# Attention feeding a mixture of experts: expert stages issued in a staggered order, and a normalization moved from VectorE to ScalarE

## The chip, the cores and the metric

The kernel runs on one core of a Trainium2 chip. A core has TensorE (PE in the profile; its weight loads are the row PEld), VectorE (DVE), ScalarE (ACT), GpSimd (POOL), SyncE (SP, which here only issues transfers) and 16 DMA engines. Engines run in parallel; each takes its own instructions strictly in order, and waits on semaphores for what it needs. The metric is the device time of one execution in microseconds (us), lower is better. One execution is profiled; the others are only timed.

## The reference, cut to what matters

First an attention with 8 batches, 8 heads, 576 positions and 64 channels: a coarse attention on positions averaged in groups of four, repeated four times, plus a local one in a band of |i-j| < 4. Then each of the 4608 tokens (512 channels) goes through the two matrices of its own expert, one of 8.

```python
out_d = sm_attn(q_d, k_d, v_d)                # means over 4 positions
out_up = np.repeat(out_d, factor, axis=2)
...
return (out_up + out_local).astype(np.float32)

def _moe_ref(x, domain_id, w1, w2):           # N, D, E, F = (4608, 512, 8, 1024)
    for e in range(E):
        mask = domain_id == e
        h = np.maximum(x[mask] @ w1[e], 0.0)
        out[mask] = h @ w2[e]
```

## The kernel before

**Routing** (lines 81 to 126, then 148 to 154). Every token gets a position in a list with 768 places per expert. Thirty-six indirect transfers on POOL's queue write the list to DRAM (`hx_idx`). Places that stay empty point at a row of zeros.

**Attention** (`_attn_head_pair`, 32 calls: 8 batches by 4 pairs of heads). POOL's queue loads q, k and v and casts them to fp16 on the way; SP's queue loads v in fp32 as well. PE transposes q and k (lines 260, 261) and forms the sums over four positions (lines 272, 274); copies marked `nc.any` (lines 262 to 277) go to ACT or DVE as the build decides. PE multiplies q by k, ACT takes the exponentials (lines 325 to 330), DVE applies the band mask (line 346), and PE multiplies by v, with a column of ones that yields the denominators. In lines 351 to 359 DVE takes the reciprocal of the coarse denominators (`odr`) and multiplies the coarse result `od_ps` by it, giving `odnp`: four multiplications a pair of heads, two of 128x64 and two of 16x64. ACT's queue stores `odnp` to DRAM (lines 368, 369). DVE does the same for the local part (lines 373 to 386), and SP's queue stores it to the bridge tensor `hx_bridge`. After each second batch `_od_add_pass` loads both parts, adds them on DVE and stores the sum; its transfers are on ACT's queue. In PSUM the tags `tr`, `ds` and `sx` have two buffers each. `ds` is shared in turn by the position sums (`pdt_ps`, `pdtl_ps`), the coarse scores (`pd_ps`) and the coarse results (`od_ps`), so an `od_ps` must be read before the next pair's position sums can be written.

**Experts** (lines 163 to 175). For expert e, `_moe_gather` issues on POOL's queue the loads of both weight matrices (1 MB each in fp16, read as 2 MB in fp32) and six indirect gathers of 128 tokens from `hx_bridge` into `xg`; the index tile `idxt` comes over SP's queue. `_moe_compute` has three parts: 24 PE transposes into `xt_ps` and four ACT copies into `xt` (call it T); 64 matmuls in eight groups, each group ended by an ACT Relu into `ht` (H); and six output groups of eight matmuls, each followed by an ACT copy into `o_sb` and an indirect scatter of 128 rows to the output on POOL's queue (O for the matmuls, S for the scatters; S.0 to S.5). The loop gathers for e+1, then computes e.

What is held how often: `idxt`, `xg`, `xt`, `ht` and `o_sb` have three buffers, the weights two, `h_ps` two, `xt_ps` and `o_ps` one. So gather e+3 needs the `idxt` of expert e back, which the last scatter of e still reads; the copy into `o_sb` number four waits for the first of its three buffers. All 48 scatters write the one tensor `out`, so each waits for the one before to have landed.

The order in each engine's queue is fixed when the program is built: among instructions that the builder takes to be ready, the one that comes first in the source is issued first, and others fill the gaps. So an engine's order is not simply the source order: in the profile the transposes of the next expert already lie between output groups of the current one.

Of the kernel before, what the change touches and what calls it, by code (L numbers as in the profile page):

```python
# [11 lines left out]
FP16 = mybir.dt.float16  # L12
I32 = mybir.dt.int32
AF = mybir.ActivationFunctionType
P = 128
CAPJ = 6
# [12 lines left out]
def kernel(  # L29
# [10 lines left out]
    nc = tc.nc  # L40

    B, H, S, D = q.shape
    NTOK = B * S
    DM = H * D
    E, _, F = moe_w1.shape
# [15 lines left out]
        name="h_ltri",  # L61
# [18 lines left out]
    with tc.tile_pool(name="prep_ps", bufs=2, space=bass.MemoryType.PSUM) as pps:  # L80
# [47 lines left out]
    with (  # L128
        tc.tile_pool(name="acon", bufs=1) as acon,
        tc.tile_pool(name="asb", bufs=5) as asb,  # L130
        tc.tile_pool(name="aps", bufs=1, space=bass.MemoryType.PSUM) as aps,
    ):
        id16a = acon.tile([P, P], FP16, name="id16a")
        nc.sync.dma_start(id16a[:], identh_c[:])
        mask5_s = acon.tile([P, 5, P], FP16, name="mask5_s")
        nc.sync.dma_start(mask5_s[:], mask5_c[:])

        for b in range(B):
            for hj in range(H // 2):
                _attn_head_pair(  # L140
                    nc, q, k, v, xdr, odb, b, 2 * hj,
                    asb, aps, id16a, mask5_s,
                    scale_local, scale_ds, S, D, SD, NSPAN, DM,
                )
            if b % 2 == 1:
                _od_add_pass(nc, xdr, odb, b - 1, S, SD, DM, asb)

    for t in range(NT):
        nc.gpsimd.indirect_dma_start(  # L149
            out=idxd[:],  # L150
            out_offset=bass.IndirectOffsetOnAxis(ap=pos_s[:, t : t + 1], axis=0),
            in_=tok_s[:, t : t + 1],
# [3 lines left out]
    with (  # L156
        tc.tile_pool(name="mcon", bufs=1) as mcon,
        tc.tile_pool(name="mw", bufs=2) as mw,
        tc.tile_pool(name="msb", bufs=3) as msb,
        tc.tile_pool(name="mhp", bufs=1, space=bass.MemoryType.PSUM) as mhp,  # L160
        tc.tile_pool(name="mop", bufs=1, space=bass.MemoryType.PSUM) as mop,
    ):
        id16 = mcon.tile([P, P], FP16, name="id16")
        nc.sync.dma_start(id16[:], identh_c[:])
        pre = [None] * E
        pre[0] = _moe_gather(nc, 0, moe_w1, moe_w2, xdr, idxd, mw, msb, DM, F)
        for e in range(E):
            if e + 1 < E:
                pre[e + 1] = _moe_gather(
                    nc, e + 1, moe_w1, moe_w2, xdr, idxd, mw, msb, DM, F  # L170
                )
            _moe_compute(
                nc, e, out, mhp, mop, msb, id16, DM, F, NTOK, *pre[e]
            )
            pre[e] = None


def _od_add_pass(nc, xdr, odb, b0, S, SD, DM, pool):
# [35 lines left out]
def _attn_head_pair(  # L214
# [66 lines left out]
    with nc.allow_low_precision(reason="sums of 4 fp16 pooled values"):  # L281
        nc.vector.tensor_reduce(
            out=vd65[:, :, 0:D],
            in_=vq[:].rearrange("p r hh d -> p hh d r"),
# [3 lines left out]
            out=vdl65[:, :, 0:D],  # L288
            in_=vql[:].rearrange("p r hh d -> p hh d r"),
# [33 lines left out]
    for hh in range(2):  # L323
        ed[hh] = asb.tile([P, 2, SD], FP16, name=f"ed{hh}", tag=f"ed{hh}")
        nc.scalar.activation(out=ed[hh][:, 0, :], in_=pd_ps[hh][:, 0, :],
                             func=AF.Exp, scale=scale_ds)
        nc.scalar.activation(out=ed[hh][0:16, 1, :], in_=pd_ps[hh][0:16, 1, :],
                             func=AF.Exp, scale=scale_ds)
        el[hh] = asb.tile([P, NSPAN, P], FP16, name=f"el{hh}", tag=f"el{hh}")
        nc.scalar.activation(out=el[hh][:], in_=sc_ps[hh][:], func=AF.Exp,  # L330
                             scale=scale_local)

    od_ps = [None, None]
# [15 lines left out]
    odnp = asb.tile([P, 2, 2, D], FP16, name="odnp")  # L349
    for hh in range(2):  # L350
        odr = asb.tile([P, 2, 1], FP32, name=f"odr{hh}", tag=f"odr{hh}")
        nc.vector.reciprocal(odr[:, 0, :], od_ps[hh][:, 0, D : D + 1])
        nc.vector.reciprocal(odr[0:16, 1, :], od_ps[hh][0:16, 1, D : D + 1])
        nc.vector.tensor_scalar_mul(
            odnp[:, 0, hh, :], od_ps[hh][:, 0, 0:D], odr[:, 0, :]
        )
        nc.vector.tensor_scalar_mul(
            odnp[0:16, 1, hh, :], od_ps[hh][0:16, 1, 0:D], odr[0:16, 1, :]
        )
        xl_ps[hh] = aps.tile([P, NSPAN, D + 1], FP32, name=f"xl_ps{hh}",  # L360
                             tag="sx", bufs=2)
        for t in range(NSPAN):
            nc.tensor.matmul(
                xl_ps[hh][:, t, :], pl[hh][:, t, :], vh[:, t, hh, :],
                start=True, stop=True,
            )
# [4 lines left out]
    for hh in range(2):  # L371
# [4 lines left out]
            out=xw[:, 0:4, hh, :],  # L376
# [5 lines left out]
            out=xw[0:96, 4, hh, :],  # L382
# [19 lines left out]
def _moe_gather(nc, e, moe_w1, moe_w2, xdr, idxd, mw, msb, DM, F):  # L402
    NDC = DM // P
    NFC = F // P
    w1e = mw.tile([P, NDC, F], FP16, name="w1e")
    nc.gpsimd.dma_start(w1e[:], moe_w1[e].rearrange("(dc p) f -> p dc f", p=P))  # L406
    w2e = mw.tile([P, NFC, DM], FP16, name="w2e")
    nc.gpsimd.dma_start(w2e[:], moe_w2[e].rearrange("(fc p) d -> p fc d", p=P))
    base = e * CAPJ * P
    idxt = msb.tile([P, CAPJ], I32, name="idxt")  # L410
    nc.sync.dma_start(
        idxt[:], idxd[base : base + CAPJ * P, 0].rearrange("(j p) -> p j", p=P)
    )
    xg = msb.tile([P, CAPJ, DM], FP16, name="xg")
    for j in range(CAPJ):
        nc.gpsimd.indirect_dma_start(  # L416
            out=xg[:, j, :],
            out_offset=None,
            in_=xdr[:],
            in_offset=bass.IndirectOffsetOnAxis(ap=idxt[:, j : j + 1], axis=0),  # L420
        )
    return (w1e, w2e, idxt, xg)


def _moe_compute(nc, e, out, mhp, mop, msb, id16, DM, F, NTOK, w1e, w2e, idxt, xg):
    NDC = DM // P
    NFC = F // P
    NCOL = CAPJ * P

    xt_ps = mhp.tile([P, NDC, NCOL], FP16, name="xt_ps", tag="xt_ps")  # L430
    for j in range(CAPJ):
        for u in range(NDC):
            nc.tensor.transpose(  # L433
                xt_ps[:, u, bass.ts(j, P)], xg[:, j, bass.ts(u, P)], id16[:]
            )
    xt = msb.tile([P, NDC, NCOL], FP16, name="xt")
    for u in range(NDC):
        nc.scalar.copy(out=xt[:, u, :], in_=xt_ps[:, u, :])  # L438

    ht = msb.tile([P, NFC, NCOL], FP16, name="ht")  # L440
    for fc in range(NFC):
        h_ps = mhp.tile([P, NCOL], FP32, name="h_ps", tag="h_ps", bufs=2)
        for dc in range(NDC):
            lhs = w1e[:, dc, bass.ts(fc, P)]
            nc.tensor.matmul(  # L445
                h_ps[:, 0:512], lhs, xt[:, dc, 0:512],
                start=(dc == 0), stop=(dc == NDC - 1),
            )
            nc.tensor.matmul(  # L449
                h_ps[:, 512:NCOL], lhs, xt[:, dc, 512:NCOL],  # L450
                start=(dc == 0), stop=(dc == NDC - 1),
            )
        nc.scalar.activation(out=ht[:, fc, :], in_=h_ps[:], func=AF.Relu)  # L453

    for j in range(CAPJ):
        o_ps = mop.tile([P, DM], FP32, name="o_ps", tag="o_ps")
        for fc in range(NFC):
            nc.tensor.matmul(  # L458
                o_ps[:], ht[:, fc, bass.ts(j, P)], w2e[:, fc, :],
                start=(fc == 0), stop=(fc == NFC - 1),  # L460
            )
        o_sb = msb.tile([P, DM], FP32, name="o_sb", tag="o_sb")
        nc.scalar.copy(out=o_sb[:], in_=o_ps[:])  # L463
        nc.gpsimd.indirect_dma_start(  # L464
            out=out[:],
            out_offset=bass.IndirectOffsetOnAxis(ap=idxt[:, j : j + 1], axis=0),
            in_=o_sb[:],
            in_offset=None,
            bounds_check=NTOK - 1,
            oob_is_err=False,  # L470
        )
# [30 lines left out]
```

## Time and profile before

| | |
|---|---|
| median of 6 runs | 692.96 us (689.18 to 694.49) |
| the profiled execution | 690.53 us, span 688.8 us |
| PE busy | 494.7 us, 72% |
| POOL busy | 334.7 us, 49% |
| ACT busy | 267.9 us, 39% |
| DVE busy | 237.0 us, 34% |
| mean granted TensorE clock | 0.945 of full |
| routing on PE and DVE, before the first pair of heads | 0 to 69 us |
| attention, 32 pairs of heads | 69 to 378 us |
| last additions to the bridge, first gather | 378 to 407 us |
| experts | 407 to 689 us |

A group's line gives the source line, the engine, the operation, output and input tiles, shapes and count, then busy time and mean duration, and after a second bar the idle time of the engine just ahead of these instructions with what ended it. A timeline's line gives start and duration in us, engine and line, and in brackets the idle time before and its releaser. In a list of waits each line says who waited for whom: the total in us, how many times, and the longest. ACTq and SPq mark instructions that only issue a transfer; they take their place in the engine's order.

### The profile page before, as it was taken

To read this page: it belongs to the slowest core of one execution; us is meant where nothing else is said; L and a number is where in the kernel's file an instruction comes from. 1 tells how busy PE (TensorE), PEld (TensorE's weight loads), DVE (VectorE), ACT (ScalarE), POOL (GpSimd) and SP (SyncE) were. 2 spreads that over 40 slices of the span, in tenths; PEclk is the share of its full clock that TensorE was granted. 3 is DMA by queue.
4 is the path that set the end of the run, shared out by engine and by line. 5 is a ranking of instruction groups with operands and counts; after the bars stand their busy time and mean duration, and the time that the engine had idled before them with its cause. 6 is when DMAs were issued, how large, how long until landed. Compare 5 with 4: busy or idle time off the path is not lost. (4 is left out here: it accounts for less than half of the span.)

```text
span 688.8 us, 10101 instructions
## 1 busy us (share of the span) xinstructions
PE 494.7 (72%) x3352; PEld 300.7 (44%) x3352; DVE 237.0 (34%) x1118; ACT 267.9 (39%) x528; POOL 334.7 (49%) x408
## 2 busy tenths in 40 slices
PE   1888989976997658867997029874939294867993
PEld 1777656543654435534554025441515152433441
DVE  2664455775667736668567100000000000000000
ACT  0100756435763345634664014531514241433541
POOL 9930667675976659955000255234252434343222
PEclk9999999999999999999999999996969788796997
DMA  9990669999999989999214597355565545364411
GB/s 118 180 83 1 52 86 105 149 143 144 100 143 170 152 106 85 131 201 181 34 29 111 147 211 169 99 86 138 90 137 101 122 95 88 111 113 121 92 50 53
DMA packets 226905, 77.93 MB, mean 113 GB/s; under 512 B 196609, under 2 KB 218898, under 8 KB 226836
## 3 DMA queue, kind: packets, MB, share of 16 engines
q0 software_dynamic: 133504, 46.71, 55.1%
q1 hardware_dynamic: 72100, 15.23, 12.9%
q10 hardware_dynamic: 21248, 15.35, 7.9%
q8 instruction: 26, 0.43, 0.3%
q14 instruction: 27, 0.22, 0.1%
HBM read 88.09 MB, written 23.37 MB: 162 GB/s over the span
## 5 line engine op out<-in xcount | busy, mean ns | idle before, releaser
L458 PE MATMUL o_ps<-w2e,ht 128*128 128x512 f16 x384 | 100.8, 410 | 71.1 <-ACT o_sb L463 69.7
L464 POOL DMA_INDIRECT out_dram<-o_sb,idxt x48 | 47.3, 986 | 118.1 <-ACT o_sb L463 45.1
L458 PEld LDWEIGHTS <-ht 128*128 128x128 f16 x384 | 39.7, 103 | 120.8 <-issue 88.9
L445 PE MATMUL h_ps<-xt,w1e 128*128 128x512 f16 x256 | 89.0, 394 | 1.6 <-ACT xt L438 1.0
L463 ACT COPY o_sb<-o_ps 128x512 f32<-128x512 f32 x48 | 28.1, 586 | 138.0 <-DMA out_dram<-o_sb,idxt 70.0
L416 POOL DMA_INDIRECT xg<-hx_bridge,idxt x48 | 46.3, 964 | 63.4 <-DMA idxt<-hx_idx 47.3
L449 PE MATMUL h_ps<-xt,w1e 128*128 128x256 f16 x256 | 72.1, 282 | 0.0
L230 POOL DMA_DIRECT2D vq<-in_v_dram x32 | 58.4, 1836 | 13.9 <-DVE pos_s L125 9.5
L230 POOL DMA_DIRECT2D qn<-in_q_dram x32 | 48.1, 1504 | 33.5 <-PE pdtl_ps L274 22.2
L453 ACT ACTIVATE ht<-h_ps 128x768 f16<-128x768 f32 x64 | 51.8, 811 | 29.4 <-PE h_ps L449 29.2
L149 POOL DMA_INDIRECT hx_idx<-tok_s,pos_s x36 | 37.8, 1049 | 48.9 <-DMA hx_idx<-tok_s,pos_s 44.4
L230 POOL DMA_DIRECT2D kn<-in_k_dram x32 | 50.4, 1575 | 2.3 <-PE pdtl_ps L274 2.3
L234 POOL DMA_DIRECT2D vql<-in_v_dram x32 | 41.5, 1297 | 2.4 <-DVE qt L265 1.6
L262 ACT COPY qt<-tr_ps 128x512 f16<-128x512 f16 x24 | 31.1, 1298 | 28.8 <-PE tr_ps L260 28.8
L234 POOL DMA_DIRECT2D knl<-in_k_dram x32 | 40.9, 1278 | 0.0
L445 PEld LDWEIGHTS <-w1e 128*128 128x128 f16 x256 | 25.9, 101 | 32.8 <-issue 4.7
L249 ACT CAST vh<-vn 128x640 f16<-128x640 f32 x32 | 23.1, 727 | 42.9 <-DVE vn L247 21.5
L433 PE MATMUL xt_ps<-id_6095,xg 128*128 128x128 f16 x192 | 15.7, 230 | 31.0 <-DMA xg<-hx_bridge,idxt 31.0
L438 ACT COPY xt<-xt_ps 128x768 f16<-128x768 f16 x32 | 24.0, 816 | 35.5 <-PE xt_ps L433 35.5
L117 PE MATMUL p_rank<-p_oh,ltri_s 128*128 128x8 f32 x72 | 21.4, 371 | 21.9 <-DVE p_oh L108 21.9
L406 POOL DMA_DIRECT2D w1e<-in_moe_w_dram x8 | 6.7, 844 | 62.0 <-DMA hx_bridge<-oax 62.0
L234 POOL DMA_DIRECT2D qnl<-in_q_dram x32 | 36.5, 1139 | 0.7 <-PE pdtl_ps L274 0.7
(1787 smaller groups left out, 1113.0 us busy)
## 6 DMA issues: line engine op xcount, KB each, us to landing
vn<-in_v_dram SPq DMA_DIRECT2D x64, 128.0 KB
w1e<-in_moe_w_dram POOLq DMA_DIRECT2D x8, 1024.0 KB, 8.5
w2e<-in_moe_w_dram POOLq DMA_DIRECT2D x8, 1024.0 KB, 9.9
oax<-hx_bridge ACTq DMA_DIRECT2D x36, 128.0 KB
hx_bridge<-oax ACTq DMA_DIRECT2D x36, 128.0 KB
qn<-in_q_dram POOLq DMA_DIRECT2D x32, 128.0 KB, 6.5
kn<-in_k_dram POOLq DMA_DIRECT2D x32, 128.0 KB, 6.3
vq<-in_v_dram POOLq DMA_DIRECT2D x32, 128.0 KB, 7.2
```

What stands on the lines that cost most here:

```text
L149: nc.gpsimd.indirect_dma_start(out=idxd[:], out_offset=bass.IndirectOffsetOnAxis(ap=pos_s[:, t : t + 1], axis=0), in_=tok_s[:, t : t + 1], ...
L230: nc.gpsimd.dma_start(dst[:], src[b, hA : hA + 2, 0:512, :].rearrange("h (p r) d -> p r h d", r=4),)
L234: nc.gpsimd.dma_start(dstl[:], src[b, hA : hA + 2, 512:S, :].rearrange("h (p r) d -> p r h d", r=4),)
L262: nc.any.tensor_copy(tt[:, 0:512].rearrange("w (p r) -> w r p", r=4), ps_m[:])
L416: nc.gpsimd.indirect_dma_start(out=xg[:, j, :], out_offset=None, in_=xdr[:], in_offset=bass.IndirectOffsetOnAxis(ap=idxt[:, j : j + 1], ax ...
L438: nc.scalar.copy(out=xt[:, u, :], in_=xt_ps[:, u, :])
L445: nc.tensor.matmul(h_ps[:, 0:512], lhs, xt[:, dc, 0:512], start=(dc == 0), stop=(dc == NDC - 1),)
L449: nc.tensor.matmul(h_ps[:, 512:NCOL], lhs, xt[:, dc, 512:NCOL], start=(dc == 0), stop=(dc == NDC - 1),)
L453: nc.scalar.activation(out=ht[:, fc, :], in_=h_ps[:], func=AF.Relu)
L458: nc.tensor.matmul(o_ps[:], ht[:, fc, bass.ts(j, P)], w2e[:, fc, :], start=(fc == 0), stop=(fc == NFC - 1),)
L463: nc.scalar.copy(out=o_sb[:], in_=o_ps[:])
L464: nc.gpsimd.indirect_dma_start(out=out[:], out_offset=bass.IndirectOffsetOnAxis(ap=idxt[:, j : j + 1], axis=0), in_=o_sb[:], in_offset=Non ...
```

## The change

Two things. First, `_moe_compute` is split into `_moe_phaseA` (T), `_moe_phaseB` (H) and `_moe_phaseC` (O and S), and the loop issues A of expert e, then C of expert e-1, then B of expert e; the last C follows the loop. Tiles, pools, shapes and the number of instructions stay; `ht` is now created at the end of A. Second, the four multiplications a pair that form `odnp` become ACT activations with the function Copy and the reciprocal as a scale per partition.

```diff
+        sA = [None] * E
         pre[0] = _moe_gather(nc, 0, moe_w1, moe_w2, xdr, idxd, mw, msb, DM, F)
         for e in range(E):
             if e + 1 < E:
                 pre[e + 1] = _moe_gather(
                     nc, e + 1, moe_w1, moe_w2, xdr, idxd, mw, msb, DM, F
                 )
-            _moe_compute(
-                nc, e, out, mhp, mop, msb, id16, DM, F, NTOK, *pre[e]
-            )
-            pre[e] = None
+            sA[e] = _moe_phaseA(nc, e, mhp, msb, id16, DM, F, *pre[e])
+            if e >= 1:
+                _moe_phaseC(nc, e - 1, out, mop, msb, DM, F, NTOK, *sA[e - 1])
+                sA[e - 1] = None
+            _moe_phaseB(nc, e, mhp, DM, F, *sA[e])
+        _moe_phaseC(nc, E - 1, out, mop, msb, DM, F, NTOK, *sA[E - 1])
...
-        nc.vector.tensor_scalar_mul(
-            odnp[:, 0, hh, :], od_ps[hh][:, 0, 0:D], odr[:, 0, :]
-        )
-        nc.vector.tensor_scalar_mul(
-            odnp[0:16, 1, hh, :], od_ps[hh][0:16, 1, 0:D], odr[0:16, 1, :]
+        nc.scalar.activation(
+            out=odnp[:, 0, hh, :], in_=od_ps[hh][:, 0, 0:D], func=AF.Copy,
+            scale=odr[:, 0, :],
+        )
+        nc.scalar.activation(
+            out=odnp[0:16, 1, hh, :], in_=od_ps[hh][0:16, 1, 0:D], func=AF.Copy,
+            scale=odr[0:16, 1, :],
         )
...
-def _moe_compute(nc, e, out, mhp, mop, msb, id16, DM, F, NTOK, w1e, w2e, idxt, xg):
+def _moe_phaseA(nc, e, mhp, msb, id16, DM, F, w1e, w2e, idxt, xg):
...
     ht = msb.tile([P, NFC, NCOL], FP16, name="ht")
+    return (w1e, w2e, idxt, xt, ht)
+
+
+def _moe_phaseB(nc, e, mhp, DM, F, w1e, w2e, idxt, xt, ht):
...
+def _moe_phaseC(nc, e, out, mop, msb, DM, F, NTOK, w1e, w2e, idxt, xt, ht):
```

More of the change, by code (lines that the diff above doesn't have):

```diff
@@ L440, in _moe_compute @@
     ht = msb.tile([P, NFC, NCOL], FP16, name="ht")
+    return (w1e, w2e, idxt, xt, ht)
+def _moe_phaseB(nc, e, mhp, DM, F, w1e, w2e, idxt, xt, ht):
+    NDC = DM // P
+    NFC = F // P
+    NCOL = CAPJ * P
     for fc in range(NFC):
@@ L453, in _moe_compute @@
         nc.scalar.activation(out=ht[:, fc, :], in_=h_ps[:], func=AF.Relu)
+def _moe_phaseC(nc, e, out, mop, msb, DM, F, NTOK, w1e, w2e, idxt, xt, ht):
+    NFC = F // P
     for j in range(CAPJ):
```

## The prediction

> **What bounds the kernel now.** Two stages make the time: attention (69 to 378 us) and experts (407 to 689 us). I read the granted clock (0.945; full until 450 us), the busy time by stretches, the waits of the experts' stage, then GpSimd's timeline there, and last ACT's and DVE's timelines in attention. By stretches PE is busy 124.9 of the 187.7 us from 450.5 to 638.2, at a granted clock of 0.82: it is idle a third of the time, so it does not set the pace. The waits (who, for whom: total, times, longest, in us):
>
> ```profile
> PEld L458 <- issue: 88.9, 76, 13.1
> ACT o_sb L463 <- DMA out_dram<-o_sb,idxt: 70.0, 11, 12.9
> PE o_ps L458 <- ACT o_sb L463: 69.7, 20, 12.9
> ...
> POOL xg L416 <- DMA idxt<-hx_idx: 47.3, 5, 10.2
> ```
>
> PE waits for ACT's copies into `o_sb`, those wait for scatters to land, and POOL stands five times some 10 us ahead of a gather. One period on POOL's queue:
>
> ```profile
> 488.59 1.00 POOL L464 DMA_INDIRECT out_dram<-o_sb,idxt  x1 [1.04 <-DMA out_dram<-o_sb,idxt]
> 499.76 0.99 POOL L416 DMA_INDIRECT xg<-hx_bridge,idxt  x1 [10.17 <-DMA idxt<-hx_idx]
> 501.05 0.98 POOL L416 DMA_INDIRECT xg<-hx_bridge,idxt  x1 [0.30 <-issue]
> 502.01 0.87 POOL L406 DMA_DIRECT2D w1e<-in_moe_w_dram  x1
> 503.19 1.01 POOL L464 DMA_INDIRECT out_dram<-o_sb,idxt  x1 [0.30 <-issue]
> ...
> 508.30 0.94 POOL L416 DMA_INDIRECT xg<-hx_bridge,idxt  x1 [0.30 <-issue]
> 512.17 1.00 POOL L464 DMA_INDIRECT out_dram<-o_sb,idxt  x1 [2.93 <-ACT o_sb L463]
> 515.71 0.99 POOL L464 DMA_INDIRECT out_dram<-o_sb,idxt  x1 [2.53 <-issue]
> ```
>
> The first line is expert 1's last scatter. The next gather (expert 4's) needs the `idxt` that this scatter reads, waits 10 us for it, and holds up every scatter queued behind. The six of expert 2 start at 503.19; the second comes 9 us after the first, the others 3.5 us apart. Last scatters lie at 450.52, 488.59, 526.03, 566.10, 602.48 and 638.23: a period of 37.5 us. It is a closed loop on POOL's queue, by means of five periods: last scatter to first gather 10.5 us (some 7.2 until the scatter lands behind the `w2e` load issued 2 us before it, 3.3 from SP's `idxt` issue at 457.87 to the gather at 461.19); first gather to second scatter 12.8; second to last scatter 14.2. The second scatter starts 9.9 to 10.2 us after the `w1e` load in all five, whether two or three gathers lay ahead of that load: the first scatter lands behind the weights. PE needs per expert 1.7 us for T (11 of 24 transposes take 0.78), 10.5 for H (55 matmuls took 9.05) and 10.3 for O (six times 1.72): 22.5 us, 15 below the period.
>
> In attention the pace is 9.6 us a pair (309 us for 32), and still 8.3 from 335 to 378 us, where POOL has nothing left to load: a chain through the two `ds` buffers. DVE and ACT at its end:
>
> ```profile
> 360.16 0.28 DVE L354 TENSOR_SCALAR odnp<-od_ps_5610,odr_5625 128x64 f16<-128x64 f32 x1
> 360.36 0.26 DVE L357 TENSOR_SCALAR odnp<-od_ps_5610,odr_5625 16x64 f16<-16x64 f32 x1
> ...
> 360.81 0.26 DVE L357 TENSOR_SCALAR odnp<-od_ps_5617,odr_5636 16x64 f16<-16x64 f32 x1
> ```
> ```profile
> 359.47 1.31 ACT L262 COPY kt<-tr_ps 128x512 f16<-128x512 f16 x1
> ...
> 360.53 0.39 ACT L265 COPY kt<-trl_ps 128x64 f16<-128x64 f16 x1
> 361.17 0.54 ACTq L368 DMA_DIRECT2D hx_odb<-odnp  x1
> 361.81 0.39 ACTq L369 DMA_DIRECT2D hx_odb<-odnp  x1
> 362.24 0.27 ACT L276 COPY qdt<-pdt_ps 128x128 f16<-128x128 f16 x1 [1.32 <-DVE xw L375]
> ```
>
> DVE forms `odnp` until 361.07; only then can ACT issue its store, and the next pair's `qdt` copy stands behind that.
>
> **The change, part by part.** *Staggered experts.* No instruction, buffer or dependency goes or comes; what changes is source order, hence the builder's choice between ready instructions. On PE it gives T(e), then O(e-1) with matmuls of H(e) in the gaps after its groups, then the rest of H(e). The old order already has this shape: one transpose run of 11 sits in each of the first two gaps after output groups, 5 and 4 matmuls of the next H in later ones. The new order fills the same gaps with H. As PE has 15 us to spare, that is worth nothing by itself; if the POOL loop were gone, the cover would be too, and PE's 22.5 us would count.
>
> What counts is POOL's order. Gathers for e+2 now stand in the source ahead of the scatters of e, so a ready gather goes first: I expect all six ahead of S(e).0, where before three or four came after it. And H(e) has some 28 of its 64 matmuls done in the gaps (five gaps of 5 or 6) where before it had 9, so after the last output group it ends some 3 us sooner (36 left instead of 55, at 0.165 us each). `w1e` of e+2 becomes ready at that moment. Two or three gathers went ahead of it; a gather takes 1.28 us from start to start, so 3 us is about two gathers: now I expect none or one. Then first gather to second scatter is six gathers (7.7) plus a scatter (3.5), 11.2 us with the load ahead of all gathers, and 12.3 (1.15 more for issuing the load) with one gather ahead; against 12.8 a saving of 1.6 or 0.5. I take 1.1, times five periods: **-5.5 us**.
> Bounds: if the load goes after all six gathers, 7.7 + 10.05 = 17.7 instead of 12.8: +4.9 a period, +25. If instead S(e).0 goes ahead of the first gather, it starts 7.2 us after the last scatter and `idxt` and the gathers (3.3 + 7.7 = 11) run beside it: 18.2 to the second scatter instead of 23.3, -5.1 a period, -26. My value lies nearest to the order seen.
> `w2e` moves at most by a place among the scatters; the 4.5 us that it adds to one landing (7.2, against a median of 2.7 for all scatters) are paid wherever it stands. At the start T(1) now goes ahead of O(0): 1.7 us plus copies of 2.9 us on ACT ahead of the first `o_sb`, partly beside matmuls, so the first scatter moves from 427.06 to about 430.5. The second was at 436.62, behind a `w1e` load of 425.61; 430.5 + 3.5 is earlier: zero; without that cover it would be 3.4. At the end the last scatters stay 3.5 us apart; S(7).0 started at 667.98, its predecessor of 663.13 was due to land 3.5 later: at most 1.3 to gain, which I leave out.
>
> *Normalization on ACT.* DVE loses four instructions a pair, 0.77 us (four starts 0.2 apart between 360.16 and 361.00, less a reciprocal of 0.07). ACT gains four. This form isn't in the trace. Nearest below: ACT's `ed` activations, 16x144 and 128x144 from PSUM, 0.26 and 0.29 long but 0.17 to 0.19 from start to start, four for 0.72 us. Above: the 128x64 copies of line 265, 0.36 on mean, four for 1.44. I take 0.8, the activations being the same instruction with a scale.
> On the path: the products no longer wait on DVE for mask and reciprocals, and the stores follow on the same engine. In the pair before (351 us) ACT stood idle from 350.96 to 352.34, with the first reciprocal done at 350.44: four products from 350.96 and the store at 351.8 instead of 352.34, 0.5 gained, provided that the second reciprocal (351.98) moves up as DVE has less ahead of it. In the pair shown ACT is in a 1.31 us copy until 360.92; products for the first `od_ps` end near 361.3 instead of 360.62, 0.65 lost for PE's next position sums behind that buffer. DVE's local part and the store to the bridge come up to 0.77 sooner in both. Between -0.5 and +0.65 a pair, I take -0.12 with DVE's relief: times 32, **-4 us**, ends -16 and +21. Queued behind a late reciprocal on ACT: exponentials, `qt` and `kt` copies, and the loads of the addition passes. The `nc.any` copies can move to DVE in return (23 of the 32 `kt` copies are ACT's), and I count zero for that; they take 1.29 us on DVE, 1.30 on ACT.
>
> One rule speaks against this part. The Trainium skill, "ScalarE: Activation LUTs", section "Rules for kernel authors", wants multiplications on VectorE and budgets about 0.3 us per ACTIVATE plus 0.83 ns per element. That would be an estimate of 0.35 us for 64 elements, 1.4 a pair and 0.6 more than I take, +20 us were all of it on the path; for 144 elements it gives 0.42, and the trace's 0.29, with the next start after 0.19, is shorter.
>
> **The sum.** -5.5 - 4 = -9.5 on the profiled execution's 690.5: 681. The median of runs lies 2.4 above that execution: **684 us**.
>
> **The rivals.**
> A. *Scatter ahead of the wait.* S(e).0 precedes the `idxt` wait and the weights travel beside it: -26, with attention's -4: 663. For it: the scatter is ready early (`o_sb` copies at 492 us, scatter at 503). Against: gathers now come first in the source, and went first even when they did not.
> B. *ACT's queue becomes the bound of attention* (the slower side). If products queue behind copies of 1.3 us in most pairs, +0.65 times 32 is +21; with -5.5 from the experts, 708. For it: ACT already stalls up to 9.7 us on the addition passes' loads, and then `od_ps` would stay held too, which it did not while DVE read it. Against: ACT's mean load in attention is 26 of 50 us, DVE's 34. It decides from 0.17 us a pair on, where it cancels the experts' 5.5.
> C. *The weights last*: all six gathers ahead of `w1e`, +25 - 4: 714. Against: H ends sooner, not later.
> D. *Nothing moves*: the builder's orders stay as they are where it matters: 690 to 695, 693.
>
> **How the numbers follow.** Forecast 0.42, own range 676 to 692; A 0.13, B 0.22, C 0.08, D 0.15. Half a per cent, 3.5 us, is about what can be told from no change: 689.5 to 696.4 counts as same. Faster: 0.36 of the forecast's case and A, and a little of D, 0.50; same: the rest of these, 0.19; slower: B and C with a mild form of them, 0.31. The range reaches to A and short of B's end: 662 to 707 leaves out C and half of B's upper part.
>
> **What would show it.** Right: the waits for `idxt` remain five of about 10 us; on POOL `w1e` stands ahead of the second gather, all six gathers ahead of the next expert's first scatter; period near 36.5; scatters 3.5 apart; attention ends at 370 to 376. Wrong: a first scatter ahead of the gathers (A), a period above 38 (C), ACT waiting for `odr` and PE for ACT's `odnp`, and attention ending after 385 (B).

## The result: half a per cent slower

The changed kernel takes 695.38 us (median of ten runs, 693.21 to 699.6) where the kernel before takes 691.3 (median of twenty) beside it. The ratio is 1.0065, with a 95% interval from 1.0036 to 1.0095. The profiled execution of the changed kernel took 696.47 us (span 694.6), 5.9 more than the 690.53 of the one before.

Two sums of opposite sign stand behind this. Cut at the issue of the first weight load, which lies behind the last attention store, attention and everything ahead of it became shorter by 6.0 us (391.66 to 385.66), and the experts longer by 11.8 (297.1 to 308.9). The prediction had -4 for the first and -5.5 for the second.

**The experts.** The chain that ended last is so cut up that its largest line is 2% of the span; I pass it by. The waits of the experts' stage, 380 us to the end (who, for whom: total, times, longest, in us):

```profile
ACT o_sb L476 <- DMA out_dram<-o_sb,idxt: 100.4, 14, 17.0
PEld L471 <- issue: 96.7, 68, 16.0
PE o_ps L471 <- ACT o_sb L476: 79.5, 14, 15.8
...
POOL xg L421 <- DMA idxt<-hx_idx: 40.4, 5, 10.1
```

The wait for `idxt` is shorter than before (40.4 us, was 47.3). Yet everything that stands behind the scatters waits longer: ACT's copies into `o_sb` 100.4 us, where it was 70.0. So the loop through POOL's queue takes longer, though the wait in it that the profile names does not. One period on POOL's queue shows why:

```profile
474.87 0.97 POOL L477 DMA_INDIRECT out_dram<-o_sb,idxt  x1 [2.51 <-issue]
475.83 0.98 POOL L413 DMA_DIRECT2D w2e<-in_moe_w_dram  x1
478.36 1.01 POOL L477 DMA_INDIRECT out_dram<-o_sb,idxt  x1 [1.55 <-ACT ht L463]
486.74 0.98 POOL L477 DMA_INDIRECT out_dram<-o_sb,idxt  x1 [7.37 <-ACT ht L463]
487.69 0.85 POOL L411 DMA_DIRECT2D w1e<-in_moe_w_dram  x1
496.00 1.00 POOL L421 DMA_INDIRECT xg<-hx_bridge,idxt  x1 [7.46 <-DMA idxt<-hx_idx]
497.31 0.97 POOL L421 DMA_INDIRECT xg<-hx_bridge,idxt  x1 [0.30 <-issue]
...
502.34 0.95 POOL L421 DMA_INDIRECT xg<-hx_bridge,idxt  x1 [0.30 <-issue]
503.59 1.01 POOL L477 DMA_INDIRECT out_dram<-o_sb,idxt  x1 [0.30 <-issue]
507.59 1.00 POOL L477 DMA_INDIRECT out_dram<-o_sb,idxt  x1 [2.99 <-ACT o_sb L476]
```

The scatter of 486.74 is the last one of an expert. The `w1e` load, 1 MB, is issued right behind it, ahead of all six gathers; before, it came after two or three of them. `w2e` is issued ahead of the last two scatters instead of the last one, and the 8.4 us gap now lies between those two. SP's timeline has the load of the indices that the gather of 496.00 waits for:

```profile
488.96 0.36 SPq L416 DMA_DIRECT2D idxt<-hx_idx  x1
```

It is issued 2.2 us after the last scatter, when that has landed, and 1.3 us after `w1e`. The gather that needs it starts 7.0 us later. In the kernel before, the gather of 499.76 that the prediction shows had its load issued here:

```profile
496.82 0.36 SPq L411 DMA_DIRECT2D idxt<-hx_idx  x1
```

There the same 3 KB took 2.9 us. The five closed periods of both kernels, as means in us:

| part of the period | before | after |
|---|---|---|
| last scatter to SP's issue of `idxt` | 7.47 | 3.12 |
| issue of `idxt` to first gather | 2.99 | 6.77 |
| first gather to second scatter | 12.82 | 11.59 |
| second to fifth scatter | 10.52 | 11.25 |
| fifth to last scatter | 3.73 | 8.39 |
| sum | 37.53 | 41.12 |

The two lines in which `w2e` is paid give 3.73 + 7.47 = 11.20 before and 8.39 + 3.12 = 11.51 after: its delay has only changed its place. (The changed kernel's five periods hold six of these delays, as the first expert's `w2e` still stood ahead of its last scatter; the other's hold five.) First gather to second scatter has become 1.2 us shorter. The step that costs is the second line, +3.8 us on the mean of five. The whole period is 3.6 longer, +17.9 in five. At the end 5.9 come back: from expert 5's last scatter to the end of the span it is 50.57 us before and 44.7 after, mostly because the delay from expert 7's `w2e` (4.7 us) is now paid ahead of that scatter, within the five periods, and no longer behind it. 17.9 - 5.9 is 12.0, and 11.8 was measured.

**Attention.** ACT's timeline around the moved products:

```profile
342.12 1.27 ACT L265 COPY qt<-tr_ps 128x512 f16<-128x512 f16 x1
343.14 0.30 ACT L357 ACTIVATE odnp<-od_ps_5448,odr_5463 128x64 f16<-128x64 f32 x1
343.33 0.29 ACT L361 ACTIVATE odnp<-od_ps_5448,odr_5463 16x64 f16<-16x64 f32 x1
343.81 0.31 ACT L357 ACTIVATE odnp<-od_ps_5455,odr_5474 128x64 f16<-128x64 f32 x1 [0.19 <-PE xl_ps_5479 L368]
344.02 0.29 ACT L361 ACTIVATE odnp<-od_ps_5455,odr_5474 16x64 f16<-16x64 f32 x1
344.15 0.33 ACTq L373 DMA_DIRECT2D hx_odb<-odnp  x1
```

A product is 0.29 to 0.31 us long, and the next starts 0.19 to 0.21 after it has started: 0.8 a pair, and the store follows at once. But the products moved something else with them. The groups by operation and tile size in attention, 68 to 380 us (busy us and mean ns, then idle time before them and its releasers), are for the kernel before

```profile
L262 ACT COPY qt<-tr_ps 128x512 f16<-128x512 f16 x24 | 31.1, 1298 | 28.8 <-PE tr_ps L260 28.8
L262 ACT COPY kt<-tr_ps 128x512 f16<-128x512 f16 x23 | 30.0, 1306 | 5.4 <-PE tr_ps L260 5.4
...
L262 DVE COPY kt<-tr_ps 128x512 f16<-128x512 f16 x9 | 11.5, 1282 | 1.6 <-PE tr_ps L260 1.6
L262 DVE COPY qt<-tr_ps 128x512 f16<-128x512 f16 x8 | 10.3, 1287 | 8.5 <-PE tr_ps L260 8.5
```

and for the changed one

```profile
L265 DVE COPY kt<-tr_ps 128x512 f16<-128x512 f16 x24 | 30.8, 1282 | 1.8 <-PE tr_ps L263 1.7
...
L265 DVE COPY qt<-tr_ps 128x512 f16<-128x512 f16 x17 | 21.8, 1281 | 3.5 <-POOL qt L271 1.8 <-PE tr_ps L263 1.7
...
L265 ACT COPY qt<-tr_ps 128x512 f16<-128x512 f16 x15 | 19.3, 1289 | 28.7 <-PE tr_ps L263 28.7
...
L265 ACT COPY kt<-tr_ps 128x512 f16<-128x512 f16 x8 | 10.5, 1308 | 3.3 <-PE tr_ps L263 3.3
```

The `nc.any` copies, whose engine the builder chooses, went the other way: of 64 large copies ACT has 23 instead of 47, and of the 64 `qdt` and `kdt` copies 10 instead of 40. ACT gave away more (24 x 1.3 = 31 us of large copies alone) than it took (32 x 0.8 = 26): its busy time fell from 267.9 to 253.4 us while DVE's rose from 237.0 to 253.8. The normalization was moved to the scalar engine; the load, taken together, was moved off it.

### The profile page after: what moved, and what is told of

Same layout as the page of the kernel before. It is cut to its first block, busy times and chain, and to the rows that moved or that the text cites. A ratio compares the mean times of both kernels' runs of the same rounds, so it can differ in the third digit from the quotient of the medians.

```text
span 694.6 us, 10093 instructions
## 1 busy us (share of the span) xinstructions
PE 485.6 (70%) x3352; PEld 295.4 (43%) x3352; DVE 253.8 (37%) x1095; ACT 253.4 (36%) x551; POOL 334.0 (48%) x408
## 5 line engine op out<-in xcount | busy, mean ns | idle before, releaser
L477 POOL DMA_INDIRECT out_dram<-o_sb,idxt x48 | 47.3, 985 | 136.9 <-ACT o_sb L476 59.7
L476 ACT COPY o_sb<-o_ps 128x512 f32<-128x512 f32 x48 | 28.5, 593 | 155.4 <-DMA out_dram<-o_sb,idxt 100.4
L421 POOL DMA_INDIRECT xg<-hx_bridge,idxt x48 | 46.0, 959 | 57.5 <-DMA idxt<-hx_idx 40.4
L459 PE MATMUL h_ps<-xt,w1e 128*128 128x256 f16 x256 | 70.1, 278 | 0.0
L233 POOL DMA_DIRECT2D qn<-in_q_dram x32 | 50.2, 1569 | 36.6 <-PE pdtl_ps L277 23.8
L233 POOL DMA_DIRECT2D vq<-in_v_dram x32 | 56.2, 1756 | 11.2 <-DVE pos_s L125 8.1
L233 POOL DMA_DIRECT2D kn<-in_k_dram x32 | 54.2, 1694 | 7.8 <-PE pdtl_ps L277 7.7
L252 ACT CAST vh<-vn 128x640 f16<-128x640 f32 x32 | 23.0, 724 | 60.7 <-DVE vn L250 22.1
L237 POOL DMA_DIRECT2D knl<-in_k_dram x32 | 44.3, 1385 | 0.0
L237 POOL DMA_DIRECT2D vql<-in_v_dram x32 | 43.3, 1362 | 0.8 <-DVE vdl_1361 L290 0.4
L263 PE MATMUL tr_ps<-id16a,kn 128*128 128x128 f16 x128 | 23.1, 299 | 26.6 <-DVE qt L265 23.7
L437 PE MATMUL xt_ps<-id_6095,xg 128*128 128x128 f16 x192 | 13.4, 230 | 33.8 <-DMA xg<-hx_bridge,idxt 33.8
L263 PE MATMUL tr_ps<-id16a,qn 128*128 128x128 f16 x128 | 25.7, 296 | 13.2 <-DVE kt L265 7.5
```

What stands on the lines that cost most here:

```text
L233: nc.gpsimd.dma_start(dst[:], src[b, hA : hA + 2, 0:512, :].rearrange("h (p r) d -> p r h d", r=4),)
L237: nc.gpsimd.dma_start(dstl[:], src[b, hA : hA + 2, 512:S, :].rearrange("h (p r) d -> p r h d", r=4),)
L263: nc.tensor.transpose(ps_m[:, r, :], nat[:, r, :, :], id16a[:])
L421: nc.gpsimd.indirect_dma_start(out=xg[:, j, :], out_offset=None, in_=xdr[:], in_offset=bass.IndirectOffsetOnAxis(ap=idxt[:, j : j + 1], ax ...
L459: nc.tensor.matmul(h_ps[:, 512:NCOL], lhs, xt[:, dc, 512:NCOL], start=(dc == 0), stop=(dc == NDC - 1),)
L477: nc.gpsimd.indirect_dma_start(out=out[:], out_offset=bass.IndirectOffsetOnAxis(ap=idxt[:, j : j + 1], axis=0), in_=o_sb[:], in_offset=Non ...
```

## The experiments

Three questions: does each part do alone what it does in the whole; why does the index load take four microseconds longer; and which of the two moves, products or copies, shortens attention.

**The parts alone.** `attn_only` is the old expert loop with the four products on ACT:

```diff
-        nc.vector.tensor_scalar_mul(
-            odnp[:, 0, hh, :], od_ps[hh][:, 0, 0:D], odr[:, 0, :]
-        )
+        nc.scalar.activation(
+            out=odnp[:, 0, hh, :], in_=od_ps[hh][:, 0, 0:D], func=AF.Copy,
+            scale=odr[:, 0, :],
+        )
...
```

> The kernel before with the four products a pair on ScalarE, the experts' loop as before. Theory: the normalization gained 6 us (the first weight load starts at 385.7 us in the changed kernel's profile, at 391.7 before), so 6 us faster than before, about 685 us, and the experts' period stays 37.5 us. Rival: it gained nothing by itself and the whole loss is spread over both parts; then 691.

684.17 us against 697.76; ratio 0.9811 [0.9749, 0.9873]. First weight load at 389.82, period 37.3. `moe_only` is the mirror image, the staggered loop with the products on VectorE:

```diff
-            _moe_compute(
-                nc, e, out, mhp, mop, msb, id16, DM, F, NTOK, *pre[e]
-            )
-            pre[e] = None
+            sA[e] = _moe_phaseA(nc, e, mhp, msb, id16, DM, F, *pre[e])
+            if e >= 1:
+                _moe_phaseC(nc, e - 1, out, mop, msb, DM, F, NTOK, *sA[e - 1])
+                sA[e - 1] = None
+            _moe_phaseB(nc, e, mhp, DM, F, *sA[e])
...
```

> The kernel before with the experts' loop staggered, the products on VectorE as before. Theory: the experts alone lose 10 to 12 us, so about 702 us, with a period of 41 us between last scatters. Rival: the loss comes from attention's changed order; then 691.

709.66 us; ratio 1.0188 [1.0123, 1.0253]. First weight load at 399.43, period 40.8. So by the medians one part is worth -13.6 us on this chip and the other +11.9, or -1.9% and +1.9% by the ratios. Of the -13.6, 9.6 lie ahead of the first weight load (389.82 against 399.43 with the products on VectorE); that the experts were also 3 us shorter than in the first profile before (293.9 against 297.1) is not explained. To see whether the parts simply add, the changed kernel and the one before were run again later, unedited, both on one other chip.

> The changed kernel itself, on the chip of these runs. Theory: the two parts add, so 684 + 12 of the experts, 696, the same as the kernel before here (698) within 1 per cent, with attention 10 us shorter and the experts 12 us longer. Rival: the parts interact (the experts lose less after the shorter attention): 690 or less.

702.38 us against 696.25; 1.0083 [1.0052, 1.0113]. First weight load at 387.56, period 41.9.

> The kernel before, for its profile on the same chip: by the theory its first weight load starts at about 400 us (391.7 in the first profile, 399 and 401 in the two kernels here that kept the products on VectorE), and the experts last as long as in the first profile, 297 us. Rival: its attention is as in the first profile, 392; then the gain of 13 us of the products alone lies elsewhere.

700.05 us in a single run, first weight load at 400.60, period 37.3. Attention -13.0 us, experts 313.2 against 297.7, +15.5. That the parts simply add is not excluded and not shown: the two ratios multiplied give 0.9995, about 0.9% either way, and the whole measured 1.0065 and 1.0083. The experts' period goes with the loop: between 40.8 and 41.9 in the three profiles with the staggered one as it is, and 36.8 to 37.5 in the eight with the old one. Attention's gain is twice that of the first pair of profiles (-6.0). The difference lies in the kernel before: its first weight load came at 391.66 there and at 400.60 here, while the changed kernel's came at 385.66 and 387.56.

**Why the index load is late: pieces or neighbour?** `idxt` is read in 768 pieces of 4 bytes. If the pieces queue one by one behind the weights, larger pieces must help. `after_idx_rows` reads 128 pieces of 24 bytes (another six tokens per partition, the same set of them):

```diff
-        idxt[:], idxd[base : base + CAPJ * P, 0].rearrange("(j p) -> p j", p=P)
+        idxt[:], idxd[base : base + CAPJ * P, 0].rearrange("(p j) -> p j", p=P)
```

> The changed kernel, with idxt read as six neighbouring indices per partition: 128 pieces of 24 bytes instead of 768 of 4 bytes. GpSimd's order is the same. Theory: the index load is slow (7.0 us from SP's issue to the first gather, before 2.9) because its many pieces queue beside the w1e load that now goes ahead of it; with a sixth of the pieces it takes 3 to 4 us, the period falls by some 3.5 us to 37.5 and the time by 17 to about 678. Rival: it is held up whatever its pieces (the engines are full for the 8 us of the weights); then 7 us stay and the time stays at 695.

694.71 us against 697.76; 0.9975 [0.9932, 1.0018]. Issue of `idxt` to gather took 5.9, 6.7, 6.8, 6.5 and 6.4 us, and the period 40.2. Even the half microsecond that the last four seem to save (7.0 to 7.3 before) is no saving, as SP issued them that much later. Counted from the issue of `w1e`, in these four periods the gather starts after 8.2 to 8.7 us here and after 8.3 to 8.7 in the changed kernel: the number of pieces is not the cause. The shorter period comes from behind the gather (first gather to second scatter 11.1 instead of 11.6, second to fifth scatter 10.8 instead of 11.25).

Then the neighbour itself was taken away. `after_keep_w1` loads no `w1e` for experts 2 to 7 and uses an earlier one in its place; `after_keep_w2` does the same with `w2e`:

```diff
-    w1e = mw.tile([P, NDC, F], FP16, name="w1e")
-    nc.gpsimd.dma_start(w1e[:], moe_w1[e].rearrange("(dc p) f -> p dc f", p=P))
+    if old is not None:
+        w1e = old
+    else:
+        w1e = mw.tile([P, NDC, F], FP16, name="w1e")
+        nc.gpsimd.dma_start(w1e[:], moe_w1[e].rearrange("(dc p) f -> p dc f", p=P))
```

> The changed kernel without the w1e loads of experts 2 to 7 (the w1e of experts 0 and 1 is used again, so the results of experts 2 to 7 are those of other weights). Theory: without w1e beside it the index load takes 2.9 us as before, and the first scatter lands in 2.7: period 35 to 36 instead of 41.1, about 667 us. Rival (the prediction's step: w1e ahead of the gathers costs nothing because it travels during the wait): the wait for idxt stays as it is and the period falls by less than 1 us, 691 or more.

681.83 us in a single run. Issue of `idxt` to gather: 2.9, 2.9, 2.9, 3.1, 2.9. One of them on POOL, and on SP:

```profile
480.10 1.00 POOL L483 DMA_INDIRECT out_dram<-o_sb,idxt  x1 [1.11 <-ACT ht L469]
490.38 1.00 POOL L427 DMA_INDIRECT xg<-hx_bridge,idxt  x1 [9.27 <-DMA idxt<-hx_idx]
```
```profile
487.48 0.36 SPq L422 DMA_DIRECT2D idxt<-hx_idx  x1
```

From 487.48 to 490.38: without `w1e` the load is back at the old 2.9 us. The profile's wait, 9.27, is longer than the changed kernel's 7.46 in the same period, because here `w2e` is again issued just ahead of the last scatter and delays its landing by the usual amount; that wait alone would have told the story the wrong way round. With the period at 36.3, this is the old loop's period, and a little less.

> The changed kernel without the w2e loads of experts 2 to 7 (the w2e of experts 0 and 1 is used again, so the results of experts 2 to 7 are those of other weights). Theory: w2e costs 4.5 to 5 us a period by holding up one scatter, wherever it stands; the fifth scatter then lands in 2.7 us, period 36, about 670 us. Rival: another load fills the gap and the period stays above 39.

677.06 us in a single run, period 35.5, so 5.6 us of the changed kernel's period go to `w2e`. This run holds the contrast within one kernel. In its first period the gather went ahead of `w1e`, in the others `w1e` went first. POOL, both cases:

```profile
448.08 0.97 POOL L483 DMA_INDIRECT out_dram<-o_sb,idxt  x1 [2.49 <-DMA out_dram<-o_sb,idxt]
453.06 0.99 POOL L427 DMA_INDIRECT xg<-hx_bridge,idxt  x1 [4.01 <-DMA idxt<-hx_idx]
454.04 0.85 POOL L414 DMA_DIRECT2D w1e<-in_moe_w_dram  x1
```
```profile
479.36 0.97 POOL L483 DMA_INDIRECT out_dram<-o_sb,idxt  x1 [2.40 <-ACT ht L469]
480.97 0.81 POOL L414 DMA_DIRECT2D w1e<-in_moe_w_dram  x1 [0.64 <-PE o_ps L477]
490.15 1.00 POOL L427 DMA_INDIRECT xg<-hx_bridge,idxt  x1 [8.37 <-DMA idxt<-hx_idx]
```

SP issues the two index loads at 450.14 and 481.61. The first takes 2.9 us to the gather; the second, 0.6 us behind a `w1e`, takes 8.5. The other three such periods have 7.8, 7.7 and 7.8. Same kernel, same load, same queues; only the `w1e` load ahead of it differs. That settles the second question.

The Trainium skill has a line for this, "DMA: Bandwidth & Descriptors", section "Issuing engines are not separate DMA queues": transfers started by the scalar, sync or gpsimd engine run on the same 16 DMA engines and interleave. The runs agree: a load on SP's own queue takes 2.9 us alone and 7 to 8.5 beside one that POOL started 0.6 to 1.4 us before. Its section "Queues, rings and completion order" says further that a completion signal lands only after every earlier write of the same DMA engine, whatever the queue. That would make a 3 KB load wait for weights, however few its pieces are. The changed kernel's trace fits: the `w1e` loads of 487.69, 527.98 and 567.62 landed after 7.9, 8.2 and 7.9 us, and each time the gather started 0.4 us after that. But no run here separates this from plain sharing of the engines.

**Take the wait away instead.** If the index load of an expert need not wait for an earlier expert's last scatter, it can be issued long before, and the loop on POOL's queue is open. `after_idx8` gives `idxt` eight buffers, one per expert:

```diff
-    idxt = msb.tile([P, CAPJ], I32, name="idxt")
+    idxt = msb.tile([P, CAPJ], I32, name="idxt", tag="idxt", bufs=8)
```

> The changed kernel with eight buffers for idxt, so that no gather waits for the last scatter of the expert three before. Theory: the loop through idxt is gone, the period is six scatters (21) plus what the two weight loads add (4.7 and some 5): 31 to 32 us, time about 650. Rival: the scatters behind one another and the weights already fill the period; above 680.

655.27 us against 697.75; 0.9379 [0.9333, 0.9425]. This beats both kernels. The period is 29.3 us. POOL's queue from one expert's fifth scatter on:

```profile
542.23 0.97 POOL L477 DMA_INDIRECT out_dram<-o_sb,idxt  x1 [2.52 <-ACT ht L463]
543.19 0.98 POOL L413 DMA_DIRECT2D w2e<-in_moe_w_dram  x1
545.62 1.01 POOL L477 DMA_INDIRECT out_dram<-o_sb,idxt  x1 [1.45 <-DMA out_dram<-o_sb,idxt]
546.64 0.82 POOL L411 DMA_DIRECT2D w1e<-in_moe_w_dram  x1
553.38 0.99 POOL L477 DMA_INDIRECT out_dram<-o_sb,idxt  x1 [5.92 <-DMA out_dram<-o_sb,idxt]
558.81 0.98 POOL L477 DMA_INDIRECT out_dram<-o_sb,idxt  x1 [4.44 <-ACT o_sb L476]
```

By then all gathers have been issued (the last at 527.17). In the three periods before, six gathers still go out between an expert's last scatter and the next one's second, but none waits for its indices. In the period shown the next expert's first scatter follows 7.8 us after the last one of its predecessor instead of 16.9 (486.74 to 503.59 in the changed kernel). From 450 to 600 us PE is busy 126.7 of 150 us, against 91.8 in the changed kernel, and its granted clock is 0.97 against 0.80. How much of the gain is the clock's was not separated. Not all of 5 x 11.8 = 59 us arrives in the total. First weight load to end of span falls from 308.9 to 264.8, 44 us: the first expert's last scatter comes 9.2 us later after the first weight load (67.8 against 58.65), since gathers of later experts stand ahead of it, and the ending takes 50.4 instead of 44.7.

Is the staggering worth anything once this wait is gone? `attn_idx8` is the old loop with the products on ACT and eight `idxt` buffers.

> Products on ScalarE, the experts' loop as before, eight idxt buffers and nothing else changed. Against the staggered loop with eight buffers (0.938 of before). Theory: once no gather waits for a scatter, the staggered loop keeps the scatters closer: this kernel is 3 to 8 us slower than that, 0.945 to 0.950. Rival: the other changes of the earlier run (six o_sb buffers, indices by rows) cost that; then 0.938 here too.

663.08 us against 696.25; 0.9524 [0.949, 0.9559], period 30.4. By the ratios to the kernel before, the same edit takes 2.9% from the old loop (`attn_only` at 0.9811), and 7% from the staggered one (1.0065 and 1.0083). And then the staggered loop is the faster by 1.5%, 0.9379 against 0.9524, with intervals that do not meet; but these two ran on different chips, and the next two runs give 0.8%, with intervals that do. From 450 to 600 us PE is busy 119.9 us here, at a clock of 0.94: in these three kernels the busier PE had the higher clock. What remains ahead of the scatters is the landing of weights beside them, and copies that wait for a free `o_sb`. More buffers for these were tried on both loops, together with the eight `idxt` and the indices by rows:

```diff
-        o_sb = msb.tile([P, DM], FP32, name="o_sb", tag="o_sb")
+        o_sb = msb.tile([P, DM], FP32, name="o_sb", tag="o_sb", bufs=6)
```

> The kernel before with the products on ScalarE, the old experts' loop, eight buffers for idxt, six for o_sb and the indices read by rows. Theory: same bound as with eight idxt buffers in the staggered loop, 31 to 32 us a period, so the staggering is worth nothing once the wait is gone: 645 to 652. Rival: the staggered order is what makes the wait's absence useful; then 10 us or more slower than that.

661.57 us; 0.9483 [0.9433, 0.9532], period 29.7. That is between theory and rival.

> The staggered loop with eight idxt buffers and six for o_sb. Theory: matmuls then never wait for a scatter of the same expert, but the scatters behind one another stay the bound: within 3 us of the run with three o_sb buffers. Rival: PE's waits for o_sb were part of the chain; 10 us faster.

655.16 us; 0.9411 [0.938, 0.9442], period 29.0. On each of the two chips the staggered kernel is ahead, by 6 us (655.27 and 661.57) and by 8 (655.16 and 663.08). Neither is a gain over three `o_sb` buffers that can be told from none: ACT's wait for a free `o_sb` was not the bound. That the scatters themselves are, one after another into the same tensor, is an inference: `after_idx8`'s POOL waits 33.7 us for an earlier scatter to land, and no run did the scatters in another way.

**What shortens attention.** One theory was that the store had kept ACT's queue waiting for DVE's products. `store_on_sp` is the kernel before with the two stores a pair on SP's queue:

```diff
-    nc.scalar.dma_start(odbv[b, 0:P, hA : hA + 2, :], odnp[:, 0, :, :])
-    nc.scalar.dma_start(odbv[b, P:SD, hA : hA + 2, :], odnp[0:16, 1, :, :])
+    nc.sync.dma_start(odbv[b, 0:P, hA : hA + 2, :], odnp[:, 0, :, :])
+    nc.sync.dma_start(odbv[b, P:SD, hA : hA + 2, :], odnp[0:16, 1, :, :])
```

> The kernel before, with the two stores of odnp issued by SP instead of ScalarE, products on VectorE. Theory: ScalarE stood behind the wait of these stores for the products; taking them off its queue gives most of the 6 us that the move of the products gave: 686. Rival: the gain came from VectorE's and ScalarE's load (products and copies changed places), then 691; the stores on SP could even stand ahead of the bridge's stores and cost something, 693.

699.54 us against 697.75; 1.0018 [0.9989, 1.0046], first weight load at 400.61. Taking that wait off ACT's queue was worth nothing, with whatever the stores cost on SP's.

Next, products and copies were moved separately. The four `pin` kernels have the old expert loop and give every `nc.any` copy in attention a fixed engine by a fixed pattern, with as many of every four pairs on ACT as the old build had (`old`: `qt` 3, `kt` 3, `qdt` 3, `kdt` 2) or about as the new one had (`new`: 2, 1, 0, 1), and the products on DVE or ACT:

```diff
+        on_act_t = (hA // 2) % 4 < (3 if tt is qt else 3)
+        on_act_d = (hA // 2) % 4 < (3 if tt is qt else 2)
+        copy_t = nc.scalar.copy if on_act_t else nc.vector.tensor_copy
+        copy_d = nc.scalar.copy if on_act_d else nc.vector.tensor_copy
...
-        nc.any.tensor_copy(
+        copy_t(
```

> The kernel before with the copies of lines 262 to 277 fixed to engines in nearly the counts that the build chose before (of 32 each on ScalarE: qt 24, kt 24, qdt 24, kdt 16), products on VectorE. A control: 0 to 1 per cent from the kernel before.

> The same fixed copies, products on ScalarE. Theory A (the gain came from copies changing to VectorE): no gain over the control, or a loss, as ScalarE now has both: 0 to 10 us slower. Theory B (the products themselves: od_ps read sooner and VectorE's chain shorter): 5 to 12 us faster than the control.

> Copies fixed in nearly the counts of the changed kernel (on ScalarE: qt 16, kt 8, qdt 0, kdt 8), products on VectorE. Theory A: 5 to 12 us faster than the control. Theory B: no gain, or a loss as VectorE now has both.

> Copies fixed in nearly the counts of the changed kernel, products on ScalarE: close to the run with the products alone moved, 13 us faster than the kernel before, under both theories; clearly less would mean that the build's choice pair by pair matters, not the counts.

| copies on ACT | products | us | ratio to before | first weight load |
|---|---|---|---|---|
| old shares | DVE | 703.89 | 1.008 [1.0044, 1.0116] | 403.82 |
| old shares | ACT | 728.13 | 1.0428 [1.039, 1.0466] | 429.2 |
| new shares | DVE | 723.56 | 1.0355 [1.0316, 1.0394] | 426.76 |
| new shares | ACT | 706.65 | 1.0112 [1.0072, 1.0152] | 409.44 |

The control, old shares and products on DVE, is 5 us above the kernel before: the fixed pattern by itself costs that. From there, the products alone cost 24 us and the copies alone 20; both together cost 3. Both theories fell, that of the products as the gain and that of the copies as the gain. What the runs show is that the two moves do not add: each alone costs 20 to 24 us, both together 3. It is not the balance of the load. Up to the first weight load ACT and DVE are busy 163 and 201 us in the control, 190 and 176 with the products alone moved, 120 and 238 with the copies alone, 147 and 213 with both: the most even of the four is the slowest. The waits from 69 to 378 us say where each move is felt. PE's wait for ACT's `qt` copies, with old shares, products on DVE (the control) and then on ACT:

```profile
PE tr_ps L264 <- ACT qt L266: 13.0, 3, 7.2
```
```profile
PE tr_ps L264 <- ACT qt L266: 32.6, 5, 9.6
```

In the opposite corner, new shares and products on DVE, ACT is the one left idle, for scores from PE; the control and that run:

```profile
ACT el L334 <- PE sc_ps L317: 16.9, 16, 3.7
```
```profile
ACT el L334 <- PE sc_ps L317: 69.3, 23, 9.6
```

What makes PE late there is not shown.

The gain of 10 to 13 us has been seen only where the builder chose the copies anew, pair by pair, with the products on ACT. A fixed pattern with nearly the same shares does not have it. What that choice does better stays open; the builder also chose each small copy by itself, which the pattern ties to the large one (of the 64 small copies behind `qt` and `kt`, 41 were on ACT before and 48 are with the old shares, 14 after and 24 with the new). The profiles show where it falls. The 32 pairs come in four batches of eight, with an addition pass between. From the first to the eighth store of a batch (issue on ACT, the first of the two), and from there to the next batch's first, in `before_again` and `after_again`, in us:

| | four batches | three passages between |
|---|---|---|
| before | 60.8, 61.5, 69.6, 59.8 | 20.9, 19.3, 15.1 |
| after | 55.6, 54.6, 54.2, 51.9 | 22.1, 24.1, 26.8 |

Within the batches 35.4 us are gained, 7.7 us a pair instead of 9.0, and half of that, 17.7, is given back at the addition passes; another 4.7 go ahead of the first store and behind the last. With the new shares fixed and the products on ACT the batches take 64.8, 62.8, 62.5 and 60.6.

## Why the prediction was wrong

*What bounds the kernel* was right: the closed loop on POOL's queue, through `idxt`, sets the experts' period. Opening it took 7% from the changed kernel. That attention hangs on a chain through the two `ds` buffers was not tested. The order of PE's matmuls was put at nothing as long as the loop is closed; staggered experts came to be worth something, 0.8 to 1.5%, only once it was open.

*POOL's order* came as predicted, at its early end: all six gathers ahead of the next expert's first scatter, `w1e` ahead of all gathers.

*First gather to second scatter, -1.1 a period*: right, -1.2.

*`w2e` is paid wherever it stands*: right, 11.20 against 11.51 us in sum, though it moved behind another scatter.

*The sum -5.5 for the experts* was the step that failed. Its saving comes from issuing `w1e` ahead of the gathers, and I counted that only from the first gather on. The time from the last scatter to the first gather was left at 10.5 us, "7.2 until the scatter lands" and 3.3 for the index load (2.99 on the mean of the five). But the index load is on the path between the two, and its price came from a kernel in which no weights were issued just ahead of it. With `w1e` issued 1 us after the last scatter it took 6.77 instead of 2.99, +3.8 a period. A cost that I had traced for a scatter ("the first scatter lands behind the weights") was not carried over to the index load that the same move put in the same place. That the stretch still measured 9.9 us is luck: `w2e`'s delay had left it for the step before, as the prediction allowed ("paid wherever it stands"). The sum should have been about -1.2 + 3.8, +13 in five periods; with second to fifth scatter (+0.7) and `w2e` (+0.3) the period showed +3.6, +17.9.

*The end, at most 1.3 to gain*: that gap, from expert 6's last scatter to expert 7's first, fell by 2.0 (4.85 to 2.87). Most of the 5.9 that came back is the last `w2e` delay, 4.7, which now falls within the five periods. *The start, zero*, was right (58.86 and 58.65 from the first weight load to the first expert's last scatter).

*Normalization on ACT, 0.8 a pair*: right. *-4 us in sum*: -6.0 in the first profiles, and -10 and -13 on the chips of the later runs. That -4 lies near -6 is luck, as it did not come by the mechanism that I gave. The store's wait for DVE, which was to go, was worth nothing (`store_on_sp`). That "The `nc.any` copies can move to DVE in return", for which I counted zero, was the mis-sized term: 24 of 64 large copies moved, and with fixed copies the same products cost 24 us instead of gaining 4. What came near was the bound of +21 for the products alone.

*The rivals.* B, ACT's queue as the bound of attention, comes nearest to what the products do alone with the copies held fast; in the kernel as built the copies moved out of the way. C predicted a period above 38, and that sign was seen, but its cause was not: C has the weights after the gathers, and they came before. A, a scatter ahead of the wait, did not occur. The time of 695 lay nearest to D, in which nothing moves; the runs have two parts of 12 to 14 us against each other.

*What would show it.* The waits for `idxt`, "five of about 10 us", were seen as five with 40.4 in sum. This could not tell right from wrong, since the wait begins at the last scatter's end on POOL and so held both the landing, now shorter, and the index load, now longer. The split at SP's issue tells them apart.

## What to carry to other kernels

When a large transfer is moved earlier, list every small transfer on the critical path that now travels beside it, on whatever queue, and price each of them with the nearest case that had such a neighbour; its duration in the quiet trace is the lower end. Where a closed loop through a buffer sets the pace, first ask what it costs to open it: here one tile of 3 KB with eight buffers was worth 3 to 7%, and the new order of the work within the closed loop cost 2%. Where the builder may choose an engine for some operations, moving others by hand can move these too (24 of 64 here), so the forecast has to be made with the new choice, not with the old one; the busy times of the two engines alone did not tell which of four kernels was fast.

## What was not expected of the hardware

A 3 KB load on SP's queue takes 2.9 us from issue to the first instruction that uses it, and 7.0 to 8.5 when a 1 MB load that POOL started is 0.6 to 1.4 us ahead; with a sixth of the pieces, issued half a microsecond later, it ends at the same time behind that load.

The unedited kernel before ended attention 9 us later in its second profile than in its first (first weight load at 400.60 and 391.66); 6.7 of the 9 lie in the passages between the batches. With the products on ACT and the copies left to the builder this point stayed between 385.7 and 390.0 in every run. What differed was not looked for.

ACT's small activations from PSUM, 128x64 at 0.30 us, let the next one start after 0.19 to 0.21, so that four of them cost 0.8 us and not 1.2.
